# Array-mode runs of a linear-attention kernel: two per pair of heads in place of five

## The chip, the core and the metric

The kernel runs on one core of a Trainium2 chip. TensorE (PE in the profile) does matrix products into PSUM, VectorE (DVE), ScalarE (ACT) and GpSimd (POOL) do the elementwise work, and SyncE (SP) and ScalarE issue the DMAs that move data between HBM and the on-chip memory. The metric is the device time of one execution in microseconds (us).

## What is computed

The reference first runs gated linear attention over 4 batches, 8 heads, 768 tokens and 48 features per head:

```python
for t in range(S):
    state = alpha[:, :, t, :, None] * state + np.einsum('bhd,bhe->bhde', k[:, :, t], v[:, :, t])
    y[:, :, t] = np.einsum('bhd,bhde->bhe', q[:, :, t], state)
```

The heads are then laid side by side as rows of 384 features (`x`), and each batch goes through a Fourier mixing and a two-layer network:

```python
X = np.fft.fft(np.fft.fft(x, axis=1), axis=2)
u = x + np.real(X)
un = (u - mu) / np.sqrt(var + 1e-06)          # layer norm over 384 features
return u + np.maximum(un @ w_ch1, 0.0) @ w_ch2   # w_ch1: 384x1536, w_ch2: 1536x384
```

## The kernel before

**Attention.** Two heads make a pair; head 0 lies on partitions 0 to 47, head 1 on 64 to 111. A batch has four pairs, and 768 tokens are six chunks of 128. For each pair eight stages are written (`attn_stages`, s1 to s8). s1 to s3 are VectorE's: two scans along the tokens give the running products of alpha and of their inverse (`w`, the tile `A`, and `al`), and two multiplications put q into `w` and k into `al`. s4 transposes five chunks of the keys (`kt`). s5 makes the scores: per chunk and head one product of 48 rows of k with q, 128x128, into PSUM; in batch 0 VectorE masks them, in batches 1 to 3 ScalarE copies them out (line 895) and GpSimd masks them. s6 makes the key products: `kt` with the values `vn`, 48x48 per chunk and head, which VectorE scales and scans and ScalarE copies to `tt`, of which there is one. s7 makes the reads: scores with values and q with `tt`, in two halves of three chunks (h2 = 0 and 1), each into one PSUM tile that ScalarE copies to `y`. s8 combines pairs for the mixing.

**Array modes.** TensorE's array is used in three ways. The products of the network, the mixing and the transposes use all of it (here: full mode). The scores have only 48 rows to contract, so the two heads run beside each other in the two row halves (row mode). The key products and the reads have outputs of 48 to 64 columns and use the two column halves (column mode). A stretch of products in one of the latter two modes is called a run here. Per pair there are five: scores h2 = 0, scores h2 = 1, key products, reads h2 = 0, reads h2 = 1.

**Network.** A batch is two blocks of 384 tokens. Per block there are 12 slices of the hidden layer; a slice is 9 products of the first layer into one of two PSUM tiles `f1` (`f<-x,wt` in the profile), a relu on ScalarE, a subtraction on VectorE, and 9 products of the second layer into three PSUM tiles `f2` (`f<-wt,h`). That makes 432 products of 128x384 per batch. The layer inputs `x` come from a normalised block by 9 transposes (`a<-cst,f`) and one copy and one subtraction for each third.

**PSUM.** There are three tiles `a`, two `f1` and three `f2`. After the start the attention and the mixing take their tiles from the three `a`.

**Order.** Every instruction is first recorded (line 614 issues them all, so the profile shows that line for nearly everything), with a key: `plan.key`, replaced through the table `PLACE` (line 211, used at 305). `Plan.emit` then places the recorded instructions engine by engine with modelled durations: among those that can start it takes the one with the smallest key, with allowances. So `PLACE` sets how attention, mixing and network interleave; each engine executes its list in order. `plan.run` ties the products of a run together so that nothing is placed between them, `plan.both` makes an instruction claim a further PSUM tile. Where the plan sees TensorE idle in the first 220 us it puts in products of zeros (line 1408, `f<-zero`), here called fillers. SyncE's DMAs keep the order in which they are recorded.

The network of batch n and the attention and mixing of batch n+1 are interleaved on TensorE; batch 0's attention and mixing come first, and the network of batch 3 is last, alone.

## Time and profile before

| | us |
|---|---|
| median of 3 runs | 495.57 (495.26 to 497.22) |
| the profiled execution | 497.96 |
| its span | 496.2 |
| TensorE busy | 484.6 (98%) |
| VectorE busy | 318.3 (64%) |
| ScalarE busy | 205.6 (41%) |
| GpSimd busy | 46.9 (9%) |

The span is the time from the first to the last instruction in the trace, and all durations come from this one execution. "Busy" of TensorE counts fillers and products that wait in the array, so 98% is not a measure of useful work. The granted clock is the share of full speed (2.4 GHz) that the chip gave TensorE; half of it is 1.2 GHz. In a timeline a row gives the start, the duration, the engine, the source line, the operation with output and inputs, how many instructions were merged, and in brackets the idle time before. A float32 product shows as two instructions, one of the network as one. Where the text needs the time from one piece of work to the next it takes the difference of two starts, since the products overlap.

### The profile page before, as it was taken

To read this page: it belongs to the slowest core of one execution; us is meant where nothing else is said; L and a number is where in the kernel's file an instruction comes from. 1 tells how busy PE (TensorE), PEld (TensorE's weight loads), DVE (VectorE), ACT (ScalarE), POOL (GpSimd) and SP (SyncE) were. 2 spreads that over 40 slices of the span, in tenths; PEclk is the share of its full clock that TensorE was granted. 3 is DMA by queue.
4 is the path that set the end of the run, shared out by engine and by line. 5 is a ranking of instruction groups with operands and counts; after the bars stand their busy time and mean duration, and the time that the engine had idled before them with its cause. 6 is when DMAs were issued, how large, how long until landed. Compare 5 with 4: busy or idle time off the path is not lost.

```text
span 496.2 us, 10674 instructions
## 1 busy us (share of the span) xinstructions
PE 484.6 (98%) x4522; PEld 451.6 (91%) x4522; DVE 318.3 (64%) x615; ACT 205.6 (41%) x418; POOL 46.9 (9%) x70
## 2 busy tenths in 40 slices
PE   9999999999999999999999999999999999999993
PEld 8989689988989987888999999889999999999993
DVE  7999998988678997861999416762767114113111
ACT  2397838677583226644313315553115112111110
POOL 0000300320222000212200001121200000000000
PEclk9999999999999997999999999999999999999998
DMA  8996304423718010532611001200201001001001
GB/s 304 402 400 250 89 3 135 161 69 107 272 67 234 1 48 1 163 145 92 186 64 49 1 0 49 90 27 10 90 1 49 0 1 49 0 1 48 1 0 54
DMA packets 20981, 46.05 MB, mean 93 GB/s; under 512 B 1920, under 2 KB 11008, under 8 KB 20800
## 3 DMA queue, kind: packets, MB, share of 16 engines
q1 hardware_dynamic: 19872, 42.81, 24.6%
q0 software_dynamic: 768, 2.37, 1.9%
q8 instruction: 37, 0.61, 0.5%
q10 hardware_dynamic: 288, 0.13, 0.1%
q14 instruction: 16, 0.13, 0.1%
HBM read 38.22 MB, written 7.08 MB: 91 GB/s over the span
## 4 chain that ended last, share of the span: by engine, by line
PE 91%; ACT 4%; DVE 2%; DMA 1%; issue 1%; SPq 0%; ACTq 0%
PE f L614 66%; PE a L614 21%; PE f L1408 4%; DMA al<-in_alpha_dram 1%; DVE y L614 1%; ACT f L614 1%; ACT b L614 1%; ACT tt L614 1%; ACT wt L614 0%; ACT y L614 0%; ACT h L295 0%; ACT x L614 0%; ACT kt L614 0%; DVE f L614 0%; DVE st L614 0%
## 5 line engine op out<-in xcount | busy, mean ns | idle before, releaser
L614 PE MATMUL f<-x,wt 128*128 128x384 f32 x864 | 177.5, 343 | 0.6 <-ACT x L614 0.4
L614 PE MATMUL f<-wt,h 128*128 128x384 f32 x864 | 173.5, 340 | 0.4 <-ACT h L295 0.4
L614 PEld LDWEIGHTS f<-x,wt 128*128 128x128 f32 x864 | 149.5, 188 | 4.4 <-ACT x L614 1.2
L614 PEld LDWEIGHTS f<-wt,h 128*128 128x128 f32 x864 | 149.8, 188 | 3.2 <-ACT h L295 0.7
L614 DVE SCALAR_TENSOR_TENSOR h<-f,h 128x384 fp32r<-128x384 f32 x96 | 53.0, 554 | 110.0 <-ACT h L295 109.5
L295 ACT ACTIVATE h<-f 128x384 fp32r<-128x384 f32 x96 | 47.1, 492 | 158.5 <-PE f L614 151.0
L614 POOL TENSOR_SCALAR_AFFINE_SELECT w<-w 128x384 f32<-128x384 f32 x48 | 31.7, 676 | 222.1 <-ACT w L614 222.1
L614 ACT COPY w<-a 128x384 f32<-128x384 f32 (+4 forms) x60 | 27.0, 481 | 31.8 <-PE a L614 31.6
L614 DVE TENSOR_TENSOR_SCAN w<-al,d 112x773 f32<-112x773 f32 (+1 forms) x17 | 28.2, 1667 | 3.9 <-PE a L614 2.6
L614 PE MATMUL a<-w,al 64*128 64x128 f32 (+1 forms) x288 | 29.4, 293 | 0.7 <-DVE tc L614 0.4
L614 PEld LDWEIGHTS a<-w,al 64*128 64x128 f32 (+1 forms) x288 | 23.2, 190 | 6.8 <-issue 1.5
L614 DVE TENSOR_TENSOR_SCAN al<-al,back 112x773 f32<-112x773 f32 (+1 forms) x17 | 28.8, 1692 | 0.1
L614 PE MATMUL a<-vn,w 128*64 128x64 f32 x576 | 27.8, 225 | 0.0
L1408 PE MATMUL f<-zero 128*32 128x48 f32 x516 | 26.6, 216 | 1.0 <-DVE zero L614 1.0
L1408 PEld LDWEIGHTS f<-zero 128*32 128x32 f32 x516 | 24.9, 117 | 2.8 <-DVE zero L614 1.0
L614 DVE TENSOR_TENSOR y<-y,a 128x191 f32<-128x191 f32 (+3 forms) x65 | 24.7, 426 | 3.9 <-PE a L614 3.8
L614 PEld LDWEIGHTS a<-vn,w 128*64 128x64 f32 x576 | 22.8, 137 | 4.4 <-issue 4.2
L614 ACT COPY tt<-tc 64x240 f32<-64x240 f32 (+1 forms) x32 | 20.3, 635 | 9.7 <-DVE tc L614 8.4
L614 DVE TENSOR_TENSOR z<-y,y 128x576 f32<-128x576 f32 (+2 forms) x17 | 11.6, 719 | 17.7 <-ACT y L614 17.7
L614 POOL DMA_INDIRECT y<-scr,rows x12 | 14.3, 1191 | 84.8 <-DMA scr<-y 51.0
L614 PE MATMUL a<-tt,w 112*64 112x96 f32 x240 | 20.2, 246 | 0.0
L614 DVE TENSOR_TENSOR y<-y,f 128x384 f32<-128x384 f32 x30 | 15.7, 554 | 4.1 <-PE f L614 4.0
(113 smaller groups left out, 513.6 us busy)
## 6 DMA issues: line engine op xcount, KB each, us to landing
kq<-in_kq_dram SPq DMA_DIRECT2D x13, 768.0 KB, 4.6
wt<-in_w_dram SPq DMA_DIRECT2D x8, 768.0 KB, 7.5
al<-in_alpha_dram SPq DMA_DIRECT2D x15, 388.0 KB, 5.2
out_dram<-y SPq DMA_DIRECT2D x24, 192.0 KB, 2.3
vn<-in_v_dram SPq DMA_DIRECT2D x14, 304.0 KB, 3.2
wt<-in_w_dram SPq DMA_DIRECT2D x8, 384.0 KB, 5.5
scr<-y SPq DMA_DIRECT2D x4, 577.5 KB, 4.2
wt<-in_kq_dram SPq DMA_DIRECT2D x2, 768.0 KB, 10.6
```

The lines of the kernel that those rows point to most:

```text
L295: return lambda out, x: e.activation(out, x, AF.Relu)
L614: op.ins = op.fns[op.engine](*[real(a) for a in op.args], **{k: real(x) for k, x in op.kwargs.items()})
L1408: lambda tag, i: nc.tensor.matmul(warm[tag][i][0:32, 512 - FW : 512], zero.real()[:, 0:32], zero.real(), start=True, stop=True), 1.0, WARM,
```

## The change

In batches 1 to 3 all twelve score products of a pair (six chunks, two heads) are one run, into four PSUM tiles at once: the three `a` and one `f1`. The masked scores are stored by head (`X[hd]`, six chunks) instead of by half. The reads of both halves are one run too, and at its head stand the key products of the next pair (`states`), which were a run of their own; so that run claims all three `a`. For this the next pair's scans, multiplications and key transposes are recorded before the reads of the present pair; the first pair of a batch has its key products alone. s6 is divided in `states` (the products) and `moves` (scaling, scan, copies to `tt`). In all batches the key transposes claim `kt` with their first instruction. `PLACE` has new numbers for all batches, batch 0 included; in batch 0 stages and runs are written as before. No computation is added or left out.

The diff, without most of the table:

```diff
--- before.py
+++ after.py
@@ -209,29 +209,26 @@
 PLACE = {
-    -700.0: -599.988779, -599.99: -699.999284, -599.98: -599.8665, -599.97: -699.999285, -599.96: -599.873091,
...
+    -700.0: -680.167718, -600.0: -599.407686, -599.99: -680.167718, -599.98: -585.879128, -599.97: 420.03415, -599.96: -594.35826,
...
 }
 
 
@@ -317,10 +314,13 @@
                     op.free = self.region(a)[4]
                 if k == 2:
                     op.moving = a
-        if self.both is not None and name == "matmul":
-            op.slots.append(self.both.tile)
-            self.both.tile.uses += 1
+        if self.both is not None and name in ("matmul", "transpose"):
+            for x in self.both:
+                if x.tile not in op.slots:
+                    op.slots.append(x.tile)
+                    x.tile.uses += 1
             self.both = None
+        op.slots.sort(key=lambda x: x.index if x.tag else -1)
         op.name, op.half, op.mode, op.follows = name, None, None, False
         if name == "matmul":
             p0, p1 = self.region(args[1])[0:2]
@@ -870,46 +870,74 @@
             for c0, c1 in parts:
                 times(1, e["A"], 0, c0, c1)
 
+        def chunk(h2, hd, c):
+            return e["X"][hd][:, 3 * h2 + c] if b else e["X"][h2][:, hd, c]
+
         def s4():
...
                 pk = psa()
+                plan.both = [kt]
                 for a in range(a0, a1):
...
         def s5():
+            if b:
+                scores()
+                return
             e["X"] = []
             for h2 in range(2):
-                X = (w3() if b else plan.tile("x").bitcast(F32))[:, 0:S].rearrange("p (two c n) -> p two c n", two=2, c=3)
+                X = plan.tile("x").bitcast(F32)[:, 0:S].rearrange("p (two c n) -> p two c n", two=2, c=3)
                 e["X"].append(X)
                 pc = [psa() for _ in range(2)]
-                plan.both = pc[1]
+                plan.both = [pc[1]]
                 for c in range(3):
...
                 for hd in range(2):
...
                     V.tensor_tensor(
...
 
+        def scores():
+            tiles = [w3() for _ in range(2)]
+            X = [x[:, 0:S].rearrange("p (c n) -> p c n", c=NT) for x in tiles]
+            e["X"] = X
+            pc = [[psa() for _ in range(2)], [psa(), plan.tile("f1")]]
+            plan.both = pc[0] + pc[1] + tiles
+            plan.run = []
+            for c in range(NT):
+                for hd, r in HEADS:
+                    T.matmul(pc[c // 3][hd][:, c % 3 * P : (c % 3 + 1) * P], R(r, c), Aq(r, c), start=True, stop=True)
+            plan.run = None
+            for h2 in range(2):
+                for hd in range(2):
+                    xs = X[hd][:, 3 * h2 : 3 * h2 + 3].rearrange("p c n -> p (c n)")
+                    FL["ev"].copy(xs, pc[h2][hd][:, 0:DM])
+                    G.affine_select(out=xs, in_=xs, pattern=[[0, 3], [1, P]], compare_op=ALU.is_ge, fill=0.0, base=0, channel_multiplier=-1)
+
         def s6():
-            pu = psa()
-            ea = tc_.rearrange("p (e a) -> p a e", a=NT - 1)
+            states()
+            moves()
+
+        def states(claim=None):
+            pu = e["pu"] = psa()
+            if claim:
+                claim.both = claim.both + [pu]
             for a in range(NT - 1):
...
                     )
+
+        def moves():
+            pu = e["pu"]
+            ea = tc_.rearrange("p (e a) -> p a e", a=NT - 1)
             V.tensor_tensor(
                 out=tc_[0:CW].rearrange("p (e a) -> p e a", a=NT - 1), in0=pu[0:CW, 0 : (NT - 1) * D].rearrange("p (e a) -> p e a", a=NT - 1),
                 in1=mt[0:CW, None, 0 : NT - 1].broadcast_to([CW, D, NT - 1]), op=ALU.mult,
@@ -918,29 +946,45 @@
             for hd, r in HEADS:
                 A.copy(tt[r, :, hd], ea[r])
 
-        def s7():
-            X = e["X"]
+        def s7(ahead=None):
             ytiles = mixed()[0]
+            pys = []
             for h2 in range(2):
-                py = psa()
-                plan.run = [] if b else None
...
+                pys.append(psa())
+                if b == 0:
+                    reads(h2, pys[h2])
+                    take(h2, pys[h2], ytiles)
+            if b:
+                plan.both, plan.run = pys, []
+                if ahead:
+                    ahead[0](plan)
+                for h2 in range(2):
+                    reads(h2, pys[h2])
                 plan.run = None
-                yo = py[:, 0 : 6 * NV].rearrange("p (a h e) -> p a h e", a=3, h=2)[:, :, :, 0:D]
-                c0 = POS[hp]
-                FL["ev"].copy(ytiles[h2][:, :, c0 : c0 + 2 * D].rearrange("p a (h e) -> p a h e", h=2), yo)
+                for h2 in range(2):
+                    take(h2, pys[h2], ytiles)
+                if ahead:
+                    ahead[1]()
+
+        def reads(h2, py):
+            for c in range(3):
+                cc = 3 * h2 + c
+                o = c * 2 * NV
+                for hd in range(2):
+                    for r in THALF:
+                        T.matmul(
+                            py[r, o + hd * NV : o + (hd + 1) * NV], chunk(h2, hd, c)[:, r], loaded["vn", pair][:, (2 * cc + hd) * D : (2 * cc + hd) * D + NV],
+                            start=hd == 0, stop=cc == 0 and hd == 1,
+                        )
+                if cc:
+                    for r in THALF:
+                        yo = py[r, o : o + 2 * NV].rearrange("p (h e) -> p h e", h=2)[:, :, 0:D]
+                        T.matmul(yo, Aq(slice(0, CW), cc)[:, r], tt[0:CW, cc - 1], start=False, stop=True)
+
+        def take(h2, py, ytiles):
+            yo = py[:, 0 : 6 * NV].rearrange("p (a h e) -> p a h e", a=3, h=2)[:, :, :, 0:D]
+            c0 = POS[hp]
+            FL["ev"].copy(ytiles[h2][:, :, c0 : c0 + 2 * D].rearrange("p a (h e) -> p a h e", h=2), yo)
 
         def s8():
             if b == 0:
@@ -952,7 +996,7 @@
             elif hp % 2:
                 combine(*mixed(), hp // 2, FL["comb"])
 
-        return [s1, s2, s3, s4, s5, s6, s7, s8]
+        return [s1, s2, s3, s4, s5, s6, s7, s8, states, moves]
 
 
     first = {}
@@ -1287,6 +1331,9 @@
         def unit(hp, n):
             def f():
                 if hp < NP2:
+                    if n == 6 and b and hp + 1 < NP2:
+                        sts[hp][6](sts[hp + 1][8:10])
+                        return
                     sts[hp][n]()
                     if n == 0 and b * NP2 + hp > 1:
                         load_alpha(b * NP2 + hp + 2)
@@ -1294,8 +1341,11 @@
             return f
 
         order = [unit(0, 0), unit(0, 1), unit(0, 2), unit(1, 0)]
+        order += [unit(0, 3), unit(0, 5)] if b else []
         for hp in range(NP2):
             order += [
+                unit(hp, 4), unit(hp + 2, 0), unit(hp + 1, 1), unit(hp + 1, 2), unit(hp + 1, 3), unit(hp, 6),
+            ] if b else [
                 unit(hp, 3), unit(hp, 4), unit(hp + 2, 0), unit(hp, 5), unit(hp + 1, 1), unit(hp + 1, 2), unit(hp, 6),
             ]
             order += [unit(hp - 1, 7)] if b == 0 and hp else []
```

How the instructions now stand on TensorE, at three places. Tile names carry a bank and a serial number, which differ between the kernels: `a_` and `f_` are PSUM tiles, `al_` holds a pair's keys, `w_` its queries or its masked scores, `vn_` or `wt` the values.

First place: the second pair of batch 3, its scores. Before, the end of a slice of the network, the first half of the scores, the next products of the network and the beginning of the reads of the pair ahead:

```order
L614 MATMUL f_1_516_3562<-x_484_3309,wt_0_120_839 128x384 x3
L614 MATMUL a_521_3591<-w_4_465_3196,al_380_2542 128x128
L614 MATMUL a_523_3596<-w_4_465_3196,al_380_2542 128x128 x2
L614 MATMUL a_521_3591<-w_4_465_3196,al_380_2542 128x128
L614 MATMUL a_523_3596<-w_4_465_3196,al_380_2542 128x128
L614 MATMUL a_521_3591<-w_4_465_3196,al_380_2542 128x128
L614 MATMUL f_0_524_3603<-wt_0_120_839,h_517_3565 128x384 x3
L614 MATMUL f_2_525_3609<-wt_0_120_839,h_517_3565 128x384 x3
L614 MATMUL f_1_526_3614<-wt_0_120_839,h_517_3565 128x384 x3
L614 MATMUL a_527_3618<-vn_414_2808,w_0_510_3528 64x64 x8
L614 MATMUL a_527_3618<-tt_129,w_1_443_3025 64x2x48 x2
L614 MATMUL a_527_3618<-vn_414_2808,w_0_510_3528 64x64 x4
```

After, from the last products of a slice on, with the scores of the same pair:

```order
L614 MATMUL f_0_517_3563<-wt_0_135_921,h_528_3635 128x384 x3
L614 MATMUL a_544_3740<-w_4_476_3315,al_388_2631 128x128
L614 MATMUL a_545_3741<-w_4_476_3315,al_388_2631 128x128
L614 MATMUL a_544_3740<-w_4_476_3315,al_388_2631 128x128
L614 MATMUL a_545_3741<-w_4_476_3315,al_388_2631 128x128
L614 MATMUL a_544_3740<-w_4_476_3315,al_388_2631 128x128
L614 MATMUL a_545_3741<-w_4_476_3315,al_388_2631 128x128
L614 MATMUL a_546_3742<-w_4_476_3315,al_388_2631 128x128
L614 MATMUL f_0_543_3739<-w_4_476_3315,al_388_2631 128x128
L614 MATMUL a_546_3742<-w_4_476_3315,al_388_2631 128x128
L614 MATMUL f_0_543_3739<-w_4_476_3315,al_388_2631 128x128
```

The six score products of one half have become twelve in a row (the twelfth is the next row), the last four chunk products alternating between an `a` and an `f` tile, and the reads no longer come after nine products of the network.

Second place: from the last read of one pair to the key products of the next, same batch. Before, the end of the reads, the second half of the scores and the first key product (`kt`):

```order
L614 MATMUL a_532_3647<-tt_129,w_1_443_3025 64x2x48 x2
L614 MATMUL a_532_3647<-vn_414_2808,w_2_514_3546 64x64 x4
L614 MATMUL a_532_3647<-tt_129,w_1_443_3025 64x2x48 x2
L614 MATMUL a_532_3647<-vn_414_2808,w_2_514_3546 64x64 x4
L614 MATMUL a_532_3647<-tt_129,w_1_443_3025 64x2x48 x2
L614 MATMUL a_533_3668<-w_4_465_3196,al_380_2542 128x128
L614 MATMUL a_534_3669<-w_4_465_3196,al_380_2542 128x128
L614 MATMUL a_533_3668<-w_4_465_3196,al_380_2542 128x128
L614 MATMUL a_534_3669<-w_4_465_3196,al_380_2542 128x128
L614 MATMUL a_533_3668<-w_4_465_3196,al_380_2542 128x128
L614 MATMUL a_534_3669<-w_4_465_3196,al_380_2542 128x128
L614 MATMUL a_537_3681<-vn_422_2883,kt_520_3582 64x48
```

After, the last key products of the next pair and the reads of the present one behind them:

```order
L614 MATMUL a_554_3814<-vn_536_3697,kt_534_3694 48x48
L614 MATMUL a_554_3814<-vn_536_3697,kt_534_3694 64x48
L614 MATMUL a_554_3814<-vn_536_3697,kt_534_3694 48x48
L614 MATMUL a_552_3812<-vn_433_2997,w_0_541_3737 64x64 x2
L614 MATMUL a_552_3812<-vn_433_2997,w_2_542_3738 64x64 x2
L614 MATMUL a_552_3812<-vn_433_2997,w_0_541_3737 64x64 x2
L614 MATMUL a_552_3812<-vn_433_2997,w_2_542_3738 64x64 x2
L614 MATMUL a_552_3812<-tt_129,w_4_476_3315 64x2x48 x2
L614 MATMUL a_552_3812<-vn_433_2997,w_0_541_3737 64x64 x2
L614 MATMUL a_552_3812<-vn_433_2997,w_2_542_3738 64x64 x2
L614 MATMUL a_552_3812<-tt_129,w_4_476_3315 64x2x48 x2
```

The score products between the reads and the key products are gone, and the key products of the next pair now stand directly ahead of the reads, in the same mode.

Third place: the end of the network of batch 0, with the last mixing products of batch 1 (`a<-cst,w`), the transposes of its first block to be (`a<-cst,f`) and the key transposes of batch 2 (`a<-cst,al`). Before:

```order
L614 MATMUL a_319_2217<-cst,w_3_305_2111 128x96
L614 MATMUL a_319_2217<-cst,w_3_305_2111 128x95
L614 MATMUL a_319_2217<-cst,w_2_302_2095 128x96
L614 MATMUL a_319_2217<-cst,w_2_302_2095 128x97
L614 MATMUL f_0_294_2039<-wt_0_280_1935,h_316_2187 128x384
L614 MATMUL f_2_296_2044<-wt_0_280_1935,h_316_2187 128x384 x3
L614 MATMUL f_1_297_2050<-wt_0_280_1935,h_316_2187 128x384 x3
L614 MATMUL f_0_294_2039<-wt_0_280_1935,h_318_2215 128x384 x3
L614 MATMUL f_2_296_2044<-wt_0_280_1935,h_318_2215 128x384 x3
L614 MATMUL f_1_297_2050<-wt_0_280_1935,h_318_2215 128x384 x3
L614 MATMUL a_322_2251<-cst,al_188_1297 128x112 x3
L614 MATMUL a_324_2262<-cst,al_188_1297 128x112 x2
```

After:

```order
L614 MATMUL a_319_2210<-cst,w_2_302_2088 1x96
L614 MATMUL a_319_2210<-cst,w_2_302_2088 1x97
L614 MATMUL f_1_317_2203<-x_173_1195,wt_0_256_1744 128x384 x3
L614 MATMUL f_1_317_2203<-x_178_1227,wt_0_275_1873 128x384 x3
L614 MATMUL f_1_294_2036<-wt_0_285_1962,h_316_2190 128x384 x3
L614 MATMUL f_2_296_2041<-wt_0_285_1962,h_316_2190 128x384 x3
L614 MATMUL f_0_297_2047<-wt_0_285_1962,h_316_2190 128x384 x3
L614 MATMUL f_1_294_2036<-wt_0_285_1962,h_322_2229 128x384 x3
L614 MATMUL f_2_296_2041<-wt_0_285_1962,h_322_2229 128x384 x2
L614 MATMUL a_326_2257<-cst,f_325_2239 128x128
L614 MATMUL a_327_2259<-cst,f_325_2239 128x128
L614 MATMUL f_2_296_2041<-wt_0_285_1962,h_322_2229 128x384
```

Before, the four products of the third mixing tile (128 rows) stand 16 network products ahead of the end of batch 0's network, and key transposes of batch 2 follow. Now the three 128-row mixing tiles stand earlier, ahead of the piece shown (the two products that are left there have one row), and the transposes of batch 1's first block begin before batch 0's network has ended.

## Rows read from the trace of the kernel before

**Rows 1.** From the page: busy time, share of the span and instructions of each engine, and the granted TensorE clock in 40 slices of the span, in tenths.

```profile
PE 484.6 (98%) x4522; PEld 451.6 (91%) x4522; DVE 318.3 (64%) x615; ACT 205.6 (41%) x418; POOL 46.9 (9%) x70
PEclk9999999999999997999999999999999999999998
```

**Rows 2.** Busy time by stretch of the span: the stretch, its length, then for PE, PEld, DVE, ACT and POOL busy us and instructions, then the granted TensorE clock, the DMA share and GB/s.

```profile
0.00:35.00 35.00, 33.77 (x641) 31.08 (x641) 32.35 (x55) 17.66 (x38) 0.85 (x8) 1.00 0.97 366
35.00:70.00 35.00, 34.34 (x444) 26.87 (x442) 32.55 (x70) 24.05 (x42) 4.60 (x3) 1.00 0.42 146
...
160.00:180.00 20.00, 20.00 (x146) 19.56 (x146) 19.09 (x38) 4.33 (x10) 0.00 (x0) 1.00 0.04 12
...
186.00:193.00 7.00, 6.16 (x33) 5.09 (x33) 5.23 (x13) 4.96 (x10) 1.00 (x2) 0.52 0.01 2
```

**Rows 3.** Timeline of TensorE, parts of 303 to 316 us: the attention of a pair of batch 3 between network products of batch 2.

```profile
303.86 0.94 PE L614 MATMUL a<-w,al 64*128 64x128 f32 x12
304.73 0.96 PE L614 MATMUL f<-x,wt 128*128 128x384 f32 x4
305.61 0.94 PE L614 MATMUL a<-w,al 64*128 64x128 f32 x12
306.48 0.78 PE L614 MATMUL a<-vn,kt 128*64 128x48 f32 x20
307.19 0.79 PE L614 MATMUL f<-x,wt 128*128 128x384 f32 x3
...
312.30 0.69 PE L614 MATMUL a<-vn,w 128*64 128x64 f32 x16
...
313.48 0.79 PE L614 MATMUL f<-x,wt 128*128 128x384 f32 x3
314.20 0.45 PE L614 MATMUL a<-vn,w 128*64 128x64 f32 x8
...
315.55 0.94 PE L614 MATMUL a<-w,al 64*128 64x128 f32 x12
```

**Rows 4.** The chain that ended last, two of its pieces: start, duration, engine and output, instructions.

```profile
131.16 2.38 PE a L614 x68
...
385.41 102.30 PE f L614 x590
```

**Rows 5.** Timeline of TensorE at 32 us: twelve score products (24 instructions) of batch 0 in one run, followed by fillers.

```profile
32.25 1.61 PE L614 MATMUL f<-w,al 64*128 64x128 f32 x24
33.78 1.29 PE L1408 MATMUL f<-zero 128*32 128x48 f32 x26
```

**Rows 6.** Timeline of TensorE from 178 to 197 us.

```profile
178.40 1.03 PE L614 MATMUL a<-cst,w 96*128 96x96 f32 x8
179.21 3.02 PE L614 MATMUL f<-wt,h 128*128 128x384 f32 x16
182.06 0.64 PE L614 MATMUL a<-cst,al 112*128 112x112 f32 x5
183.04 0.78 PE L614 MATMUL a<-vn,kt 128*64 128x48 f32 x20 [0.34 <-ACT kt L614]
183.75 0.93 PE L614 MATMUL a<-w,al 48*128 48x128 f32 x6
...
187.86 1.30 PE L614 MATMUL a<-cst,f 128*128 128x128 f32 x3
189.09 1.33 PE L1408 MATMUL f<-zero 128*32 128x48 f32 x14
190.85 1.33 PE L614 MATMUL f<-x,wt 128*128 128x384 f32 x3 [0.42 <-ACT x L614]
...
194.02 0.51 PE L614 MATMUL a<-cst,f 128*128 128x128 f32 x3
194.28 0.78 PE L614 MATMUL f<-x,wt 128*128 128x384 f32 x3
194.90 0.49 PE L614 MATMUL a<-cst,f 128*128 128x128 f32 x3
...
196.95 0.85 PE L614 MATMUL f<-wt,h 128*128 128x384 f32 x4
```

**Rows 7.** Timelines of VectorE and then of ScalarE in the same stretch: the last additions of batch 0's network output (`y<-y,f`) and additions of batch 1's mixing (`y<-y,a`), then the scaling of batch 1's normalised rows.

```profile
181.22 1.60 DVE L614 TENSOR_TENSOR y<-y,f 128x384 f32<-128x384 f32 x3 [0.25 <-PE f L614]
182.73 1.07 DVE L614 TENSOR_TENSOR y<-y,a 128x191 f32<-128x191 f32 x3
...
186.73 3.70 ACT L614 ACTIVATE f<-y,r,r 128x384 f32<-128x384 f32 x6 [0.73 <-DVE r L614]
```

**Rows 8.** Timeline of TensorE before the first network product: fillers, then the transposes of batch 0's first block.

```profile
63.91 4.52 PE L1408 MATMUL f<-zero 128*32 128x48 f32 x102
68.59 1.17 PE L614 MATMUL f<-cst,f 128*128 128x128 f32 x9
```

**Rows 9.** From the page's groups: busy us, mean ns of one, then the idle time before.

```profile
L295 ACT ACTIVATE h<-f 128x384 fp32r<-128x384 f32 x96 | 47.1, 492 | 158.5 <-PE f L614 151.0
L614 POOL TENSOR_SCALAR_AFFINE_SELECT w<-w 128x384 f32<-128x384 f32 x48 | 31.7, 676 | 222.1 <-ACT w L614 222.1
L614 ACT COPY w<-a 128x384 f32<-128x384 f32 (+4 forms) x60 | 27.0, 481 | 31.8 <-PE a L614 31.6
```

**Rows 10.** Timeline of SyncE's DMA queue: start, and how long the issue stood there.

```profile
108.75 17.44 SPq L614 DMA_DIRECT2D wt<-in_w_dram  x4
...
127.57 0.38 SPq L614 DMA_DIRECT2D vn<-in_v_dram  x1
```

More of the change, by code (lines that the diff above doesn't have):

```diff
@@ L893, in s5 @@
                 for hd in range(2):
-                    if b >= MKB:
-                        xs = X[:, hd].rearrange("p c n -> p (c n)")
-                        FL["ev"].copy(xs, pc[hd][:, 0:DM])
-                        G.affine_select(out=xs, in_=xs, pattern=[[0, 3], [1, P]], compare_op=ALU.is_ge, fill=0.0, base=0, channel_multiplier=-1)
-                        continue
                     V.tensor_tensor(
```

13 lines of the change are left out of this document (removed), and 41 rows, old and new, of the table PLACE.

## The prediction

> **What bounds the kernel now.** First the page's busy shares: TensorE 98% of the span, VectorE 64%, ScalarE 41% [rows 1]. So the time is TensorE's, and the question is how much of its 484.6 us is work. The stretches come next. In the first 70 us VectorE is busy for 32.4 and 32.6 of 35 us [rows 2], and TensorE fills its gaps with products of zeros, 102 instructions in the last gap alone [rows 8]: this part is bound by the chain through VectorE, not by products. From there on TensorE has no gaps, except around 185 us, where the granted clock drops to 0.52 of full speed, which is the level of 1.2 GHz [rows 1, 2]. Last, the TensorE timeline with small windows, for what a change of array mode costs.
>
> The price of a mode, from starts. A network product takes 102.30 / 590 = 0.173 us in an undisturbed stretch [rows 4]. Four of them between two score runs take 305.61 - 304.73 = 0.88 where 4 x 0.173 = 0.69; three between two halves of the reads take 314.20 - 313.48 = 0.72 where 0.52 is due [rows 3]. So a visit to full mode costs 0.19 beside its products. Six score products (12 instructions) in one run take 0.87 [rows 3]; twelve in one run take 33.78 - 32.25 = 1.53 [rows 5]. Two runs instead of one thus cost 2 x 0.87 - 1.53 = 0.21 in row mode. Reads in one piece take 2.38 (68 instructions) [rows 4]; in two pieces 313.48 - 312.30 = 1.18 and 315.55 - 314.20 = 1.35 [rows 3], together 0.15 more.
>
> The gap near 185 us: batch 0's network ends at 182.06, and the interleaving with transposes of batch 1's `x` is over at 196.95, 14.9 us later [rows 6]. Ahead of it stand the four last mixing products of batch 1, which are the end of the row of 8 instructions at 178.40. In between TensorE does 5 key transposes (about 0.45, at 0.26 for three transposes, from 194.02 to 194.28), key products 0.71 (306.48 to 307.19 [rows 3]), 18 of 24 score instructions (1.2), 18 transposes and 18 network products (0.88 for three of each, from 194.02 to 194.90, so 5.3) and one change of mode, 0.2: 7.9 us of work. The remaining 7.0 are waiting and the half clock, with fillers at 189.09. The chain behind it: VectorE's last mixing additions stand behind additions for the network's output, and ScalarE's scaling starts only at 186.73 [rows 7].
>
> **The change part by part.** *Fewer runs.* In the program order, from the first network product on, the kernel before leaves full mode 43 times, with 30 runs in row mode and 30 in column mode; the changed one leaves it 28 times, with 12 and 16 (the three first pairs' key products stay alone, and one of these is cut in two). The saving is 15 x 0.19 + 18 x 0.21 + 14 x 0.15 = 2.9 + 3.8 + 2.1 = 8.7 us (a third, 2.9, in each of batches 1 to 3). It is on the path, since TensorE has no gaps there outside 182 to 197; and the last 102 us are network alone, so what is saved earlier moves the end.
>
> *The gap of 7.0 us.* Only three tiles `a` exist, and the mixing of a batch wants four: three of 128 rows and one of a single row. Before, the single row is taken early and the third 128-row tile has to wait for one to come free; both blocks of batch 1 then end late. In the changed order the single row is the one that waits (only the second block needs it), the third tile is some 40 network products (7 us) further ahead of the end of batch 0's network, and nine transposes for the first block are placed before that end. The products of batch 2's first pair that filled the gap are done later, under network work. I take 6.5 of the 7.0 as gone; the bounds are 0 (VectorE is no earlier, 19.09 of 20 us busy from 160 to 180 [rows 2]) and 7.0.
>
> *The start.* Up to the first network product stages and runs are the same but for the order, and VectorE bounds it. In the program order 242 fillers stand ahead of that product instead of 251, and 6 more right after it; at 4.52 us for 102 instructions, two per filler [rows 8], this is 0.8 less before and 0.5 more after. I take 0, with 2 us either way: a loss if the first masks come in another order than TensorE asks for, a gain of the same size if the fillers left out were idle time.
>
> *New waits.* The runs claim more at once, and nothing can pass them on TensorE's queue. The score run needs all three `a` and one `f1`, the other `f1` carries the network. After it stand 17 to 18 network products (2.9 to 3.1 us) before the next `f1`, or the last pair's reads, need what ScalarE and GpSimd empty and mask: four copies of 0.481, one relu of 0.492 and the last mask of 0.676 [rows 9], 3.1 us in series. The products thus just cover it. Where the cover fails, the cost per pair is at most a copy and a relu, about 1 us, so 0 to 12 us over twelve pairs; below zero is excluded, since these are waits that did not exist. I take 1.0 in all, near the lower end, because the masks of the second half overlap with the reads of the first.
>
> The Trainium skill speaks against the change here: its page "TensorEngine Tiling (Array Packing)", section "PSUM Bottleneck", says that tiling speeds up TensorE but not the emptying of PSUM, which may become the bottleneck. By that rule the second of the rivals below would be the likely case; by the row, ScalarE is idle for 31.6 us waiting for these very products [rows 9], and the sum stays.
>
> *Sum.* -8.7 - 6.5 + 0 + 1.0 = -14.2 us. The profiled execution took 497.96 us for a span of 496.2, and should become 483.8 for 482.0. Against the median of 495.57, which is 2.4 lower than that execution, it is 481.4.
>
> **The rivals.** *The gap stays.* The reads of a pair now wait for the next pair's scans and key transposes, and batch 1's combination on VectorE may come as late as before while batch 0's network ends earlier. For it: VectorE's 19.09 of 20 us. Against it: the order gives the first block's tiles 7 us more. Then the 2.9 us of batch 1 are lost in the gap as well: 495.57 - 5.8 = 489.8.
>
> *Emptying PSUM becomes the bound.* ScalarE, which has alpha's tests, weights and copies to `tt` in the same queue, starts the four copies late, and TensorE stands for about 0.6 us in each of twelve pairs: 7.2 in place of the 1.0, so 487.6. Against it: ScalarE is busy 41% of the span [rows 1].
>
> *Slower: the values come late.* The key products of a pair are now in the run with the reads of the pair before it, so its values `vn` are needed a pair earlier, while the buffer (two of them) comes free only after the reads before that. On SyncE's queue the issue of `vn` stands behind weight loads that held the queue for 17.44 us, from 108.75 to past 126 [rows 10]. If a run in batch 1 meets that, the reads, the combination and the mixing follow late, batch 0's network runs out, and TensorE waits: 495.57 - 8.7 + 17.4 = 504.3 with the gap included. It decides once the lateness is over 14 us; a delay of a few us is hidden by batch 0's network. Against it: in batch 1 SyncE's loads stand in the same order as before.
>
> **How the numbers follow.** The forecast 0.72, around 481.4, its own range 476 to 486. The gap stays 0.14 (489.8). Emptying PSUM 0.08 (487.6). Values late 0.06 (504.3, or less where the lateness is partly hidden). The range 476 to 490 takes in the first three cases: its lower end is the sum with the whole gap, no new waits and 2 us at the start (-17.7, 477.9) and 2 us for rounding in the switch prices, its upper end the gap's case. What a measurement of this kernel can tell from no change is 0.5%, about 2.5 us. All of the forecast is faster by more, nearly all of the first two rivals too; of the last, two thirds are slower and the rest within the bound: faster 0.92, within 0.5% 0.04, slower 0.04.
>
> **What the profile after would show.** Right: score rows of 24 instructions that take 1.5 us, key products directly followed by reads with no network product between them, no drop of the clock near 180 us, fewer or no fillers there, and the last network stretch starting 10 us or more earlier. The switch price is wrong if one run of 24 takes clearly more than 1.53. The gap's term is wrong if TensorE waits for ScalarE's `x` at the end of batch 0's network. New waits would show as idle time of TensorE before `f<-x,wt` or reads, with ScalarE's copies `w<-a` or GpSimd's masks as what ended it; late values as a wait on DMA `vn`. The forecast as a whole is wrong if the first network product starts more than 3 us later than before (70 us), since nothing later can make up for that.

## The result and the profile after

The changed kernel takes 482.95 us (median of 4 runs, 481.13 to 485.53), the kernel before 496.36 beside it: ratio 0.972, 95% interval 0.9688 to 0.9751. The profiled execution took 481.34 us for a span of 479.6, where 483.8 for 482.0 was predicted. The page after has TensorE as full as before, and a clock of nine tenths or more in every slice:

```profile
PE 468.9 (98%) x4502; PEld 443.5 (92%) x4502; DVE 319.8 (67%) x622; ACT 203.7 (42%) x411; POOL 52.9 (11%) x70
PEclk9999999999999999999999999999999999999999
```

Against [rows 1], TensorE's busy time is 15.7 us shorter, and the 7 in the 16th slice is gone. The windows, with the columns of [rows 2], show the same place:

```profile
160.00:180.00 20.00, 20.00 (x146) 19.57 (x145) 18.80 (x50) 5.58 (x12) 0.00 (x0) 1.00 0.01 2
180.00:186.00 6.00, 6.00 (x37) 5.33 (x36) 5.82 (x13) 2.79 (x7) 0.00 (x0) 1.00 0.30 98
186.00:193.00 7.00, 7.00 (x48) 6.77 (x47) 6.33 (x14) 3.52 (x9) 0.00 (x0) 1.00 0.01 2
```

TensorE is busy throughout and at 2.4 GHz, where [rows 2] had 0.52 of it from 186 to 193; VectorE is as full as before from 160 to 180. TensorE's timeline there, and then ScalarE's:

```profile
177.77 2.59 PE L614 MATMUL f<-wt,h 128*128 128x384 f32 x14
180.20 0.38 PE L614 MATMUL a<-cst,f 128*128 128x128 f32 x2
180.33 0.42 PE L614 MATMUL f<-wt,h 128*128 128x384 f32 x1
180.59 0.60 PE L614 MATMUL a<-cst,f 128*128 128x128 f32 x4
180.94 0.42 PE L614 MATMUL f<-wt,h 128*128 128x384 f32 x1
181.21 0.49 PE L614 MATMUL a<-cst,f 128*128 128x128 f32 x3
181.45 0.59 PE L614 MATMUL f<-wt,h 128*128 128x384 f32 x2
182.04 3.42 PE L614 MATMUL f<-x,wt 128*128 128x384 f32 x18
```

```profile
178.42 1.90 ACT L614 ACTIVATE f<-y,r,r 128x384 f32<-128x384 f32 x3
181.51 1.25 ACT L614 CAST x<-a 128x384 fp32r<-128x384 f32 x3 [1.20 <-PE a L614]
```

The nine transposes of batch 1's first block now lie between the last products of batch 0, and batch 1's first layer follows at 182.04, against 190.85 in [rows 6]. ScalarE scales three thirds (1.90 us) and then casts `x`; before, it scaled six in a row (3.70, [rows 7]) ahead of the first cast:

```profile
190.34 0.46 ACT L614 CAST x<-a 128x384 fp32r<-128x384 f32 x1
```

A score run and a joined run of key products and reads, on TensorE:

```profile
93.67 1.04 PE L614 MATMUL a<-w,al 64*128 64x128 f32 x13
94.45 0.27 PE L614 MATMUL f<-w,al 48*128 48x128 f32 x1
...
95.21 1.84 PE L614 MATMUL f<-wt,h 128*128 128x384 f32 x9
```

```profile
205.91 0.72 PE L614 MATMUL a<-vn,kt 128*64 128x48 f32 x19
206.43 0.26 PE L614 MATMUL a<-vn,w 128*64 128x64 f32 x1
...
208.87 0.62 PE L614 MATMUL f<-wt,h 128*128 128x384 f32 x2
```

All twelve scores take 95.21 - 93.67 = 1.54 us (1.53 was forecast from [rows 5]), and the joined run 208.87 - 205.91 = 2.96, with no network product inside.

**Where the time went.** Between the first network product and the last product both kernels issue the same instructions on TensorE (but for 14 and 12 of the fillers), so TensorE's time can be divided by adding up, over the single records of the trace, each run from its first start to the first start behind it:

| us | before | after | difference |
|---|---|---|---|
| scores (288 instructions; 30 runs, then 12) | 28.02 | 18.46 | -9.56 |
| key products and reads (1056; 30 runs, then 16) | 38.01 | 36.40 | -1.61 |
| everything else (44 stretches, then 29) | 352.25 | 347.31 | -4.94 |
| from the first to the last product | 418.29 | 402.16 | -16.1 |
| up to the first network product | 70.11 | 71.27 | +1.2 |
| from the last product to the end of the span | 7.84 | 6.19 | -1.7 |

The scores gave most, though the forecast had 3.8 us for them. TensorE's timeline of the kernel before shows why, at a half of the scores that its plan had divided by head:

```profile
97.62 0.93 PE L614 MATMUL a<-w,al 48*128 48x128 f32 x6
98.48 1.15 PE L614 MATMUL f<-wt,h 128*128 128x384 f32 x5
99.47 0.50 PE L614 MATMUL f<-x,wt 128*128 128x384 f32 x2
99.90 0.93 PE L614 MATMUL a<-w,al 64*128 64x128 f32 x6
100.76 0.45 PE L614 MATMUL f<-x,wt 128*128 128x384 f32 x1
```

Six instructions of head 0 alone take 98.48 - 97.62 = 0.86, and six of head 1 alone 100.76 - 99.90 = 0.86: each as much as the twelve of both heads in turn (0.87, [rows 3]). So in these rows the heads run beside each other in the two row halves only where their products stand next to each other. The Trainium skill, page "TensorEngine Tiling (Array Packing)", section "Tiling Modes", says that different tiles can execute in parallel; the trace agrees where the heads take turns (0.87 for twelve), and shows that it is lost with the order. No run changes that order alone, and since each head's six products also write a PSUM tile of their own, the rows do not part the row half from the tile.

As 24 undivided halves of 0.868 the scores would have taken 20.8 us. The kernel before took 7.2 more: 1.5 for waits and the half clock in the gap (its run there from 183.75 to 187.86), 5.7 for heads that did not run side by side, 1.3 of that in the gap. The step from 24 halves to 12 runs gave only 2.4.

### The profile page after: what moved, and what is told of

Its sections match the earlier page's. It is cut to its first block, busy times and chain, and to the rows that moved or that the text cites. A ratio compares the mean times of both kernels' runs of the same rounds, so it can differ in the third digit from the quotient of the medians.

```text
span 479.6 us, 10604 instructions
## 1 busy us (share of the span) xinstructions
PE 468.9 (98%) x4502; PEld 443.5 (92%) x4502; DVE 319.8 (67%) x622; ACT 203.7 (42%) x411; POOL 52.9 (11%) x70
## 4 chain that ended last, share of the span: by engine, by line
PE 84%; DVE 6%; DMA 3%; ACT 1%; issue 1%; SPq 0%; DVEq 0%; ACTq 0%
PE f L614 63%; PE a L614 19%; DMA kq<-in_kq_dram 2%; PE f L1458 2%; DVE w L614 1%; DVE al L614 1%; DMA wt<-in_w_dram 1%; DVE x L614 1%; DVE tc L614 1%; DVE wt L614 1%; DVE y L614 0%; ACT tt L614 0%; ACT h L292 0%; DVE st L614 0%; DVE h L614 0%
## 5 line engine op out<-in xcount | busy, mean ns | idle before, releaser
L614 PE MATMUL f<-x,wt 128*128 128x384 f32 x864 | 172.1, 340 | 0.0
L614 POOL TENSOR_SCALAR_AFFINE_SELECT w<-w 128x384 f32<-128x384 f32 x48 | 36.4, 792 | 224.0 <-ACT w L614 224.0
L614 ACT COPY w<-a 128x384 f32<-128x384 f32 (+4 forms) x48 | 20.6, 484 | 25.8 <-PE a L614 25.7
L614 PEld LDWEIGHTS a<-vn,w 128*64 128x64 f32 x576 | 25.6, 136 | 0.7 <-issue 0.7
L614 POOL DMA_INDIRECT y<-scr,rows x12 | 15.6, 1298 | 80.8 <-DMA scr<-y 49.5
L614 PE MATMUL a<-tt,w 112*64 112x96 f32 x240 | 22.7, 246 | 0.0
L614 ACT COPY y<-a 128x288 f32<-128x288 f32 x24 | 9.6, 401 | 27.0 <-PE a L614 26.8
L614 PE MATMUL f<-w,al 48*128 48x128 f32 (+1 forms) x168 | 19.6, 282 | 0.4 <-ACT kt L614 0.3
L614 PEld LDWEIGHTS a<-w,al 64*128 64x128 f32 x216 | 16.9, 187 | 3.0 <-issue 2.2
L614 PE MATMUL a<-w,al 64*128 64x128 f32 x216 | 19.2, 283 | 0.0
```

The lines of the kernel that those rows point to most:

```text
L614: op.ins = op.fns[op.engine](*[real(a) for a in op.args], **{k: real(x) for k, x in op.kwargs.items()})
```

## Experiments

Besides medians, a second measure is used where a few us matter: the time from the start of the 46th first-layer product (near 88 us) to that of the last product, in the profiled run. It leaves out the start and the end, which vary by themselves. It is 384.94 us in the profile above.

**The changed kernel again.** No edit.

> The changed kernel once more, as it is, beside the kernel before on one chip, as the base of the edits that follow. Its four runs so far lay at 481.13 and 481.34 and at 484.56 and 485.53 us, the latter with mean granted clocks of 0.991 and 0.989 in place of 0.998. Theory: the higher pair holds a stretch at the half clock (1.2 GHz) that the profiled run does not have; then the runs fall again into two groups some 3 to 4 us apart, by the mean granted clock. Rival: the pair differs by chance in many places; then the runs spread evenly between 481 and 486 and go with no clock. Ratio to the kernel before: 0.969 to 0.975 by either.

> The changed kernel as it is, as the base of the three edits of this call. Its ten runs so far fall into two groups, 480.7 to 482.3 us with mean granted clocks from 0.995 and 484.4 to 486.0 us with clocks up to 0.992; the same two groups again, the median somewhere between 481 and 486 as the groups fall out.

483.35 us (480.72 to 486.03), ratio 0.9728 (0.9692 to 0.9764), and 482.28 (480.83 to 485.45), ratio 0.9721 (0.9691 to 0.9752). With the first four that makes 16 runs: ten with clocks from 0.995 at 480.7 to 483.1, six with clocks up to 0.992 at 484.4 to 486.0. The two groups are there again, except that the faster ones reach 483.1. The first one's profile has a stretch of 3.4 us at 1.2 GHz near 38 us (below), and with 481.78 us it is nevertheless one of the faster ten; no run of the slower six was profiled. From the 46th product on: 384.23 in both.

**Score runs cut** in two and in three by a network product that stood behind the run:

```diff
...
+    def cut(self, n, k):
+        return n + 6 if self.ops[n].mode == "rows" and k - n == 11 else None
...
```

```diff
...
+    def cut(self, n, k):
+        return (n + 4, n + 8) if self.ops[n].mode == "rows" and k - n == 11 else ()
...
```

> The changed kernel with one 512-column product of the network moved into the middle of each of the 12 runs of scores, so that 12 score runs of 12 products become 24 of six; nothing else is moved and nothing is left out. Returns to the full array mode go from 28 to 40, row runs from 12 to 24. Theory (each return costs 0.19 us of TensorE and each row run 0.21 us, and TensorE never waits there): 12 x 0.40 = +4.8 us over the changed kernel's run of this call. Rival (the time went by the order of products and the missing waits, and a change of mode is covered by weight loads): 0 +/- 0.5 us.

> As the one before, with two products of the network in each run of scores, after the fourth and the eighth product: 36 row runs of four, 52 returns to the full mode. Theory: +24 x 0.40 = +9.6 us over the changed kernel's run of this call, twice what the cut in two costs. Rival (a change of mode is covered): 0 +/- 0.5 us. A third way: the first cut costs by the product that is moved and its consumers, and not by the mode; then the second cut adds clearly less or more than the first.

486.98 us (484.42 to 490.75), ratio 0.9808 (0.9764 to 0.9853); 492.38 (489.77 to 495.82), ratio 0.9905 (0.9876 to 0.9934). From the 46th product on 388.91 and 394.08, so +4.68 and +9.85 over the control: 0.39 and 0.41 per cut, where 0.40 was expected. The whole times are rougher: for the cut in two 3.2 us between the means of the three faster runs of each kernel and 4.6 between those of the three slower, for the cut in three 9.6 between the faster. The score runs alone grew from 18.46 to 20.84 and 23.22 us, 0.198 per cut; the rest is 0.19 to 0.21 per return to full mode. TensorE's timeline of the kernel with scores in two:

```profile
93.45 0.94 PE L615 MATMUL a<-w,al 64*128 64x128 f32 x12
94.31 0.45 PE L615 MATMUL f<-wt,h 128*128 128x384 f32 x1
94.69 0.37 PE L615 MATMUL a<-w,al 64*128 64x128 f32 x1
...
95.56 1.66 PE L615 MATMUL f<-wt,h 128*128 128x384 f32 x8
```

The one network product in the middle occupies 94.69 - 94.31 = 0.38 where it is due 0.173; both halves take 0.86 to 0.87. The rival, that a change of mode is covered, falls.

**Key products apart from the reads**, by the same rearrangement:

```diff
...
+    def cut(self, n, k):
+        return n + 10 if self.ops[n].mode == "cols" and k - n == 43 else None
...
```

> The changed kernel with one 512-column product of the network between the next pair's key products and the reads of both value halves, in the 9 runs that hold both: column runs go from 16 to 25, returns to the full mode from 28 to 37. Theory: 9 x (0.15 + 0.19) = +3.1 us over the changed kernel's run of this call. Rival (a column run costs its reads' wait for the values or the copy of keys, and not the mode): 0 +/- 0.5 us, or less than nothing where a wait inside the run goes.

484.90 us (483.69 to 485.70), ratio 0.9752 (0.9729 to 0.9775). All six runs have clocks from 0.996; their mean of 484.7 is 3.1 over the 481.6 of the control's three runs from 0.995. From the 46th product on 387.24: +3.01, of which column runs 1.22 (0.136 each) and returns 1.79 (0.20 each). As the theory had it.

**The single row first again**, and then the same without the products of zeros that fill the pause this brings:

```diff
+                    if m == 0 and scr is scratch[1]:
+                        e["p4"] = psa()
+                        dstage(e["p4"][0:1], slice(DM, DM + 1), (1, 0))
...
-                if m == 0 and not pms:
+                if m == 0 and not pms and scr is not scratch[1]:
```

```diff
-WARM = 220.0
+WARM = 170.0
```

> The changed kernel with the single-row tile of the first batch's mixing planned first again, as in the kernel before, so that one of the three 128-row tiles is the one left without an accumulator and the nine transposes of the next batch's block 0 come behind the first batch's network; the two runs of another array mode per pair stay. Theory of the gap (third 128-row tile late, so the next batch's first products stand still): +6.5 us over the changed kernel's faster group, that is 487 to 489 us, with TensorE idle for some 7 us near 180 us and a half clock behind it. Rival (the gap went since the mode runs are shorter and the mixing came earlier, wherever the single-row tile stands): 0 +/- 1 us, 481 to 486 us.

> The kernel with the single-row tile planned first, without the 38 products of zeros (76 instructions in the trace) that filled TensorE's pause between 180.56 and 185.70 us; everything else stands as it was. With them it was 2.0 to 2.7 us slower than the changed kernel, not the 6.5 forecast. Theory (the forecast's gap was about half pause and half the half clock that follows on a pause, and the zeros hold the clock): a stretch of some 7 us at the half clock from about 184 us on, as in the kernel before, and 2.5 to 3.5 us more than with the zeros: 486.5 to 488 us. Rival (the clock does not fall, or falls where TensorE waits anyway): the same as with the zeros, 484 us.

484.31 us (483.56 to 488.89), ratio 0.9771 (0.9735 to 0.9807), and without zeros 486.76 (486.25 to 487.08), ratio 0.9801 (0.9783 to 0.9820). From the 46th product on 388.07 and 389.52: +3.84 over the control, and 1.45 more. TensorE's timelines, with zeros and then without, and a window of the latter:

```profile
177.34 3.28 PE L614 MATMUL f<-wt,h 128*128 128x384 f32 x18
180.56 3.33 PE L1461 MATMUL f<-zero 128*32 128x48 f32 x74
183.82 1.53 PE L614 MATMUL a<-cst,f 128*128 128x128 f32 x9
185.28 0.27 PE L1461 MATMUL f<-zero 128*32 128x48 f32 x2
185.70 1.49 PE L614 MATMUL f<-x,wt 128*128 128x384 f32 x7
```

```profile
178.09 3.28 PE L614 MATMUL f<-wt,h 128*128 128x384 f32 x18
184.35 1.74 PE L614 MATMUL a<-cst,f 128*128 128x128 f32 x9 [2.98 <-ACT f L614]
186.44 2.61 PE L614 MATMUL f<-x,wt 128*128 128x384 f32 x7 [0.35 <-ACT x L614]
```

```profile
184.00:191.00 7.00, 6.19 (x29) 5.30 (x30) 6.47 (x13) 5.43 (x12) 0.00 (x0) 0.76 0.02 6
```

The pause comes back, but costs 3.8 us in the profile and not 6.5 (the rows of zeros hold 183.82 - 180.56 and 185.70 - 185.28, together 3.7), and 2.4 by the whole times (means of five runs from 0.995 on either side, 484.4 and 481.9). So the order of the mixing tiles is only part of the gap. The plan was made anew for this edit, so orders behind that place moved too; the two kernels shown here differ in the zeros alone. Without zeros TensorE stands for 2.98 us, its clock is then at 1.2 GHz for 3.4 us, and seven products take 2.61 in place of 1.49. The theory of the half clock is right in kind: the stretch is half of what was expected, and the price is 1.45 us by the profiles and 2.45 by the medians, where 2.5 to 3.5 was expected.

**The kernel before, kept going in its gap:**

```diff
+HELD = {1033: 5, 1046: 5, 1049: 10, 1052: 8, 1055: 14}
...
+                    count = max(count, HELD.get(sum(1 for m in order if isinstance(m, int) and ops[m].engine == "PE"), 0))
```

> The kernel before, not the changed one, with 35 more products of zeros (70 instructions in the trace) where TensorE waits near 185 us: 5 each ahead of the key products and of the second half of the scores, 10 ahead of the next scores, 8 ahead of the transposes of batch 1's first block, and 14 in place of 7 ahead of its first network product; nothing else moves. Theory (of the 7.0 us of that gap about half is the half clock, and what keeps TensorE going keeps the clock): the 6.8 us at the half clock from 186 us on go or shrink to some 3.4, and with them 1.5 to 3.5 us: 0.993 to 0.997 of the kernel before. Rival 1 (the gap is waiting for VectorE and ScalarE alone, and TensorE's clock matters to nobody there): 1.000. Rival 2 (the zeros stand in the way of scores and transposes that are ready): up to 1 us slower.

496.25 us (494.66 to 496.90) against 496.99: ratio 0.9977 (0.9962 to 0.9991). The clock no longer falls there, and still TensorE waits to the same moment:

```profile
187.85 0.87 PE L1410 MATMUL f<-zero 128*32 128x48 f32 x16
188.65 0.55 PE L616 MATMUL a<-cst,f 128*128 128x128 f32 x3
189.12 1.38 PE L1410 MATMUL f<-zero 128*32 128x48 f32 x28
190.73 0.80 PE L616 MATMUL f<-x,wt 128*128 128x384 f32 x3 [0.23 <-ACT x L616]
```

Batch 1's first product starts at 190.73 against 190.85 in [rows 6], with ScalarE's `x` as what ended the wait. So the gap before was nearly all a wait for VectorE's and ScalarE's chain, and the half clock cost 0.4 (first to last product, 417.88 against 418.29) to 1.1 us (by the ratio). The first rival is nearly right, though the interval excludes its 1.000; the theory's 1.5 to 3.5 is more than was measured, and only the far end of the interval (0.9962, 1.9 us) reaches into it.

**Zeros at 35 us**, twice:

```diff
+HELD = 163
...
+                    if sum(1 for m in order if isinstance(m, int) and ops[m].engine == "PE") == HELD:
+                        count = 12
```

> The changed kernel with 12 more products of zeros (0.043 us apart where TensorE issues them in a row) ahead of the two transposes that wait for a copy of keys near 35 us, where TensorE stands still for 0.6 us in two of the profiled runs; nothing else moves. Two of the profiled runs have 3.4 and 6.8 us at the half clock from 37.7 us on, three have none. Theory (the half clock follows on that pause, and is what separates the two groups of times): all runs in the faster group, 480.5 to 482.5 us, with clocks from 0.995. Rival 1 (the half clock has another cause): two groups as before. Rival 2 (the zeros stand in the way of the transposes): up to 0.5 us later in both groups.

> The kernel with twelve more products of zeros near 35 us once more, as the base of the run that follows. In its first five runs it lay between 482.69 and 483.24 us with clocks from 0.996, so no run of the slower group, but 1.3 us over the faster one; its profile has two new waits of TensorE, 0.57 and 0.60 us at 211 and 214 us, behind VectorE that waited 4.18 us for queries and keys (kq). If the twelve zeros brought that wait, it is there again: 482.7 to 483.3 us. If the load of kq was slow by chance, some runs come at 481 us.

482.88 us (482.69 to 483.24), ratio 0.9722 (0.9697 to 0.9746), and 482.78 (482.34 to 484.21), ratio 0.9731 (0.9707 to 0.9754). A window (columns of [rows 2]) of the control with the 3.4 us, and of the first of these:

```profile
30.00:50.00 20.00, 19.36 (x337) 17.51 (x333) 18.67 (x39) 13.72 (x23) 0.00 (x0) 0.91 0.83 311
```

```profile
30.00:50.00 20.00, 19.93 (x383) 17.93 (x379) 19.47 (x39) 14.28 (x24) 0.00 (x0) 1.00 0.85 318
```

No clock under 0.994 in these ten runs nor in the ten of the next two kernels, which have the zeros too; without them 14 of 43 runs lie at 0.992 or below (the changed kernel, the cut runs, and the single row first with its zeros). So the zeros keep both the half clock and the slower group away, as the theory has it, but the time does not come down to 481: both profiles have a new wait. VectorE and then TensorE, in the first:

```profile
208.70 0.96 DVE L617 TENSOR_TENSOR w<-kq,w 112x768 f32<-112x768 f32 x1 [4.18 <-DMA kq<-in_kq_dram]
```

```profile
211.37 0.94 PE L617 MATMUL a<-w,al 48*128 48x128 f32 x12 [0.57 <-DVE tc L617]
...
213.94 0.80 PE L617 MATMUL a<-cst,al 112*128 112x112 f32 x5 [0.60 <-ACT w L617]
```

From the 46th product on 386.10 and 386.41, some 2 us over the control. The load of `kq` took 208.70 - 202.10 = 6.6 us from its issue, against 206.62 - 201.87 = 4.8 in the second control; why it is later here stays open.

**Queries ahead of alpha** on SyncE's queue, on top of the zeros:

```diff
...
+        for k in pairs[-2:]:
+            order.remove(loads[k])
+            order.insert(order.index(loads[k - 1]), loads[k])
```

> As the one before, and two of SyncE's loads of kq (batch 2's pairs, issued at 201.55 and 211.92 us in the changed kernel's profile) stand ahead of the load of alpha behind which they waited. Theory (kq stood behind a load that waits for VectorE's scan, 0.4 us ahead of it, and came 2.2 to 4.2 us after VectorE wanted it): VectorE's waits for kq at 206 and 218 us go, and with them TensorE's waits behind them, 0.6 us in the changed kernel's profile and 1.2 in the last one's: 481.0 to 482.0 us, 1 us under the run before of this call. Rival (the load of alpha, now behind, is late in its place, or the waits come back at the next load): 0.

482.15 us (481.29 to 483.11), ratio 0.9706 (0.9685 to 0.9728). The load is issued 13 us earlier, in SyncE's queue:

```profile
188.24 0.33 SPq L623 DMA_DIRECT2D kq<-in_kq_dram  x1
201.65 0.33 SPq L623 DMA_DIRECT2D al<-in_alpha_dram  x1
```

VectorE's and TensorE's waits there are gone, and from the 46th product on it takes 384.17, 2.2 less than the run beside it. As a whole it is 0.6 us better by medians, inside the intervals: the waits went, as the theory says, but a gain over the changed kernel isn't shown.

**The rectifier first**, also on top of the zeros:

```diff
...
+        for i in (2, 2):
+            order.insert(acts[EARLY], order.pop(acts[EARLY - i]))
...
```

> As the one before, and ScalarE's rectifier at 83.97 us stands ahead of the two weight casts at 82.28 and 83.22 us, the first of which waits for its weights' DMA (1.25 us in the changed kernel's profile, 1.73 in another run's) while TensorE waits 0.81 us (1.3 in that other run) for the rectifier. Theory: that wait goes, 0.8 us less than the run before of this call, 479.7 to 481.7 us in the faster group. Rival (the casts, now 0.5 us later, make the weights late where they are first used): 0, the wait only moves.

484.07 us (483.03 to 485.45), ratio 0.9752 (0.9726 to 0.9779): not better than the zeros alone (482.88). TensorE's longest wait there, in the kernel with the zeros and then with this edit on top:

```profile
81.90 0.96 PE L617 MATMUL f<-wt,h 128*128 128x384 f32 x4 [0.85 <-ACT h L293]
```

```profile
81.92 0.97 PE L622 MATMUL f<-wt,h 128*128 128x384 f32 x4 [1.11 <-ACT h L294]
```

With the zeros the wait that the edit was for (0.81 at 84.50 in the changed kernel) was no longer there. It stood one rectifier earlier, behind a cast that waits 1.91 us for its DMA, and the edit leaves it. What the edit adds are gaps of 0.77 and 0.78 us between product starts at 87.61 and 89.17: the two casts, now behind the rectifier, hold up the scalings (87.63 instead of 85.76) and the next rectifier (89.43 instead of 87.58). So the theory was not tested, and neither was the rival; ahead of the wrong rectifier the edit only costs.

## Why the prediction was right, point by point

| us | predicted | measured |
|---|---|---|
| price of runs and returns | -8.7 | -7.3 |
| heads side by side, outside the gap | in the above, 6 runs at 0.21 | -4.4 |
| the gap near 185 us | -6.5 | -6.6 |
| new waits | +1.0 | +2.2 |
| start | 0, 2 either way | +1.2 |
| behind the last product | nothing | -1.7 |
| span | -14.2 | -16.6 |

*Fewer runs.* The prices stand: 0.20 per return, 0.198 per row run, 0.136 per column run, where 0.19, 0.21 and 0.15 were read from single rows. With 15 returns, 12 row runs and the 14 column runs (38.01 - 36.40, with a wait of 0.3 us at the end of one of them taken off) that is 3.0 + 2.4 + 1.9 = 7.3. What failed is what the sum left out: it held the order of the products inside a run at nothing, without a reason, since it took the price from two halves that were whole [rows 3] and put it on all. Six of its 18 row runs were pieces of halves divided by head, and those and three halves in one run, but not in turn, cost 4.4 us outside the gap. The table counts only the 12 runs that came of joining halves. Counted with all 18, as the forecast did, 18 x 0.198 = 3.6 stands for its 3.8, and the first three rows become -8.5, -3.1 for the order alone and -6.7.

*The gap.* The size is right: 1.5 in waits and half clock in the scores, 1.3 for heads one after the other (the forecast counted those 18 instructions as 1.2 us of work, so they were in its 7.0), and about 3.8 in transposes and products (an estimate; 4.1 with the forecast's figures for the work), from the rows at 183, 187.86 to 190.85 and 190.85 to 196.95. The cause named, the single row that now waits in place of the third 128-row tile, is worth 2.4 to 3.8 by the kernel that undoes it. Up to 1.1 is the half clock. For the rest there is a candidate in the rows, not in a run: ScalarE scaled both blocks before the first cast, and that run has it in the new order (three, then the casts).

*The start.* Inside its bounds. It was 70.6 to 71.8 in the profiles of the changed order without a low clock near 38 us.

*New waits.* Sized too low. The +2.2 are what is left: 1.9 of everything else (-4.94 = -3.0 - 3.8 + 1.9) and 0.3 at the end of a column run. The view of TensorE's waits (total, times, longest) names 1.5 of it, where the kernel before has 0.4 of the first kind:

```profile
PE f L614 <- ACT h L292: 1.2, 3, 0.8
...
PE a L614 <- DVE tc L614: 0.3, 1, 0.3
```

The largest is not where it was looked for. ScalarE's timeline:

```profile
82.28 0.91 ACT L614 ACTIVATE b<-wt 128x768 int8<-128x768 bf16 x1 [1.25 <-DMA wt<-in_w_dram]
83.22 0.84 ACT L614 ACTIVATE wt<-b 128x768 f32<-128x768 int8 x1
83.97 0.47 ACT L292 ACTIVATE h<-f 128x384 fp32r<-128x384 f32 x1
```

A rectifier stands behind a weight cast that waits for its DMA, ahead of the first score run.

*The rivals.* The gap did not stay. Emptying PSUM did not become the bound: no wait of TensorE for the copies or masks of a score run in the profile after, though GpSimd's masks grew from 676 to 792 ns [rows 9]:

```profile
L614 POOL TENSOR_SCALAR_AFFINE_SELECT w<-w 128x384 f32<-128x384 f32 x48 | 36.4, 792 | 224.0 <-ACT w L614 224.0
L614 ACT COPY w<-a 128x384 f32<-128x384 f32 (+4 forms) x48 | 20.6, 484 | 25.8 <-PE a L614 25.7
```

The rule of the Trainium skill that speaks for it, page "TensorEngine Tiling (Array Packing)", section "PSUM Bottleneck", did not decide here: ScalarE is busy 42%. Late values did not come, but their mechanism did, with `kq` in place of `vn`: VectorE waits 2.2 to 2.4 us for it near 206 us in the profiles of the changed kernel, and where it waits 2.7 (at 218.44 in the profile after) or 4.2, TensorE waits too. Such a wait is not new in itself: the kernel before has one of 2.38 us, at 214.06, which TensorE does not feel.

The median of 482.95 lies 1.5 over the 481.4 though the profiled span went 2.4 further than forecast. Two of the four runs, with mean clocks of 0.989 and 0.991, took 485.53 and 484.56; the two others are within 0.3 of the forecast. What separates them was not foreseen (last section). That the sum came so near is in part luck: the order inside the runs, for which it had no term, and 1.7 us behind the last product were gained, the start and more waits than forecast were lost, which leaves 2.4 us of gain, and the two slower runs took that back from the median.

## What to carry to other kernels

Read the order of a run's instructions, not only their number: two row halves worked at once only while their products alternated, and a planner that is free to take one head first doubles the time of those products (0.86 us for six or for twelve). A price for mode changes read from starts of the trace (product to product, with and without the run between) held within a tenth when tested by cuts. And an added wait is best looked for wherever the changed order lets an in-order queue stand on a DMA; before it is mended, look whether it is still there in the kernel that the mend goes on (the rectifier's was not).

## What was not expected of the hardware

- The kernel's times fall into two groups some 3.5 us apart, and a stretch at 1.2 GHz near 38 us goes with the slower one. Its length matters: the control's profile has 3.4 us of it, starts its first network product at 71.79 (70.55 to 71.75 in the ten profiles of the changed order without one) and is one of the faster runs; that of the scores in three has 6.8 us, starts it at 74.31 and is one of the slower. The mean clock of the slower six, 0.990 against 0.998, would be some 7 us at half clock, an estimate, since none of them was profiled. The stretch follows on about 0.6 us in which TensorE had nothing to do at 35 us (858 and 868 ns between starts); 12 products of zeros there, and no clock under 0.994 was seen in 20 runs. The same pause (865 to 871 ns) without a drop stands in four other profiles, so it is not the pause alone.
- A stretch at the half clock need not cost its length: 6.8 us of it in the kernel before cost 0.4 to 1.1, since TensorE was waiting for other engines.
- From the start of the last product to the last instruction it takes 6.1 to 6.2 us in nine profiles and 7.2 to 7.8 in five. Three of the five are of the changed order, so up to 1.6 us between two profiled executions can be chance; both profiles of the order before are among the five, so whether the change has a part in its -1.7 stays open.
